# Two groups of small attention products a unit, and 48 weight columns in the state update of later units

## The chip, the cores and the metric

The kernel runs on one NeuronCore of one Trainium2 chip. The metric is device time in microseconds, from the first to the last instruction of a run with what the device adds around it; lower is better. The core has five instruction queues that matter here: TensorE (PE, with its weight loads shown as PEld), VectorE (DVE), ScalarE (ACT), GpSimd (POOL) and SyncE (SP), which issues the DMAs. Each works off its own queue in order; semaphores tie them together.

## The reference

Two blocks follow one another, all in fp32. The first is a gated linear attention (4 batches, 8 heads, 768 steps, 48 channels a head):

```python
f = 1.0 / (1.0 + np.exp(-f_logit))
for t in range(S):
    state = f[:, :, t, :, None] * state + einsum('bhd,bhe->bhde', k[:, :, t], v[:, :, t])
    y[:, :, t] = einsum('bhd,bhde->bhe', q[:, :, t], state)
```

Its heads are laid side by side to x of 4 x 768 x 384. The second is a mixer: a low-rank product along the sequence (`u = x + (x^T U V)^T`, rank 32), then `u + relu(u @ w_ch1) @ w_ch2` with 1536 hidden channels.

## The kernel before

**Units.** The attention is computed in 16 units, each one batch and two heads (`par` 0 and 1, in partitions 0 to 47 and 64 to 111; each head has 64 places, PAD, for its 48 channels, D). A unit has 12 chunks of 64 steps. Units 0 to 3 are batch 0, 4 to 7 batch 1, 8 to 11 batch 2, 12 to 15 batch 3.

A unit n goes through two sets of steps. `prepare(n)` makes its operands, mostly on DVE and ACT: gates (transpose of f_logit, sigmoid), keep (a DVE scan from the end of each chunk, L694; the ACT copy `least`, L699, comes behind it), keys (k transposed and multiplied), read-back (a DVE scan, L712) and queries (q transposed and multiplied into qT). From unit 6 on the transposes are DVE's.

`attend(n)` does the products, with small matmuls of 48 or 64 rows and up to 64 columns, of which four can stand in the array at once:

- scores (`sc`, L788): 48 matmuls, and then DVE's multiplication with the causal mask to A (L795).
- kept (`pt`, L809): 12 transposes of the keys, copied by ACT to kb (L815); ACT also spreads the chunk decays to `whole` (L813).
- states (`ds`, L825): 48 matmuls with kb as weights (64 columns a head, of which 48 are channels) and v; ACT copies the result to `added` (L831).
- scan (L846): a DVE scan over `added` and `whole`, which carries the state from chunk to chunk; for batches 1 to 3 ACT then copies it to st in another order (L851).
- read (`y`, L863): 44 matmuls of qT with st, and a tiny ACT copy of the last columns of y to `seen` (L870).
- inner (`y`, L881): 48 matmuls of A with v onto the same y, in reverse order of blocks, so that the first of them writes what `seen` reads and has to wait for it; ACT copies y to x (L887).

**The order around the change.** `steps` yields, for n = 5 and so on, ten pieces: scores of unit n-1, kept of n, gates, keep and keys of n+1, read of n-1, states and scan of n (one piece), read-back and queries of n+1, and inner of n-1. `attention` calls a `Fill` before each piece. The fill holds the mixer work of the batch before, in pieces with a cost each, and issues them in equal portions by cost: for batch 1's units the second layer of batch 0's mixer (`po`, L283), for batches 2 and 3 the first layer (`pz`, L258: 12 full matmuls a piece, then an ACT relu, L268) and the products of a fast two by two scheme for the second layer (`pw`, L312, with DVE additions, L187). A portion need not hold a whole piece; then two small groups meet on PE.

PE's queue is in the order in which the pieces are called. DVE's and ACT's are too, up to the start of batch 1's mixer; after that a planner orders these two by priority, where the mask, the state scan and the mixer's additions are marked urgent. PSUM has three buffers of two banks for the small groups (`big`) and two of one bank for pz, po and pw (`mm`). In batch 3 `beside` also issues 14 DVE additions of weights (L743), two behind each piece from the 21st on. `start_mixer` runs between the batches: the low-rank product of the batch just finished, with what is left of the fill.

Batch 0's units have an order of their own and come before. After batch 3 the last mixer products run alone (`pp`, L410, and `pw`).

Of the kernel before, what the change touches and what calls it, by code (L numbers as in the profile page):

```python
# [21 lines left out]
PAD = 64  # L22
# [450 lines left out]
def factored_path(ctx, tc, q, k, v, f_logit, moe_U, moe_V, moe_w_ch1, moe_w_ch2, out, ok):  # L473
# [4 lines left out]
    nc = tc.nc  # L478
    B, H, S, D = q.shape
    P = nc.NUM_PARTITIONS  # L480
# [3 lines left out]
    NBL = S // P  # L484
# [45 lines left out]
    def load(n, *names):  # L530

        b, hp = divmod(n, HP)
        for nm in names:
            if nm == "v":
                v_tiles[n] = three.tile([P, NBL, 2, D], F32, name="v_nat")
            for par in range(2):
                head = src[nm][b, 2 * hp + par]
                if nm == "v" and par:

                    for s in range(2):  # L540
                        nc.sync.dma_start(
                            out=v_tiles[n][(1 - s) * C : (2 - s) * C, :, par, :],
                            in_=head.rearrange("(c s p) d -> s p c d", s=2, p=C)[s],
                        )
                    continue
                if nm == "v" or n < TURNED:
                    dst = v_tiles[n] if nm == "v" else nat[n % 2][nm]
                    nc.sync.dma_start(out=dst[:, :, par, 0:D], in_=head.rearrange("(c p) d -> p c d", p=P))
                    continue
                head = head.rearrange("(c i) d -> i c d", i=NB)  # L550
                for part in range(2):
                    p0 = par * PAD + part * NB
                    n_ch = min(NB, D - part * NB)
                    nc.sync.dma_start(
                        out=raw[n % 2][nm][p0 : p0 + NB, :].rearrange("p (c d) -> p c d", d=NB)[:, :, 0:n_ch],
                        in_=head[:, :, part * NB : part * NB + n_ch],
                    )
# [38 lines left out]
    added = const.tile([P, D * NCH + 1], F32, name="added")  # L596
# [173 lines left out]
    def attend(n):  # L770

        b, hp = divmod(n, HP)
        T = units[n]
        vt = v_tiles[n]
        rows = [slice(par * PAD, par * PAD + D) for par in range(2)]
        chunk = [slice(c * C, (c + 1) * C) for c in range(NCH)]

        part = [slice(s * C, (s + 1) * C) for s in range(2)]
# [37 lines left out]

        def states():

            ds = ps_big.tile([P, 2, 512], F32, name="ds", tag="big")
            for c in range(NBL):  # L820
                for s in range(2):
                    for par in range(2):

                        i = (c + (s & par)) % NBL
                        nc.tensor.matmul(  # L825
                            ds[par * PAD : (par + 1) * PAD, s, c * D : (c + 1) * D],
                            lhsT=T["kb"][part[s ^ par], par, i, :], rhs=vt[part[s ^ par], c, par, :],
                            start=True, stop=True,
                        )

            nc.scalar.copy(  # L831
                added[:, 1:].rearrange("p (e c s) -> p e c s", c=NBL, s=2),
                ds[:, :, 0 : NBL * D].rearrange("p s (c e) -> p e c s", e=D),
            )

        def scan():

            st = T["st"] = two.tile([P, NCH, D], F32, name="st")
            by_e = "p (e c) -> p c e"
            if b == 0:  # L840
                states = st.rearrange("p c e -> p (c e)")
                T["st"] = states.rearrange(by_e, c=NCH)
            else:
                states = added[:, 0 : D * NCH]
            with tc.high_priority(offset=AHEAD):
                nc.vector.tensor_tensor_scan(  # L846
                    states, added[:, 0 : D * NCH], T["whole"].rearrange("p e c -> p (e c)"), 0.0, ALU.add, ALU.mult
                )
                if b > 0:

                    nc.scalar.copy(st, states.rearrange(by_e, c=NCH))  # L851
# [20 lines left out]
        def inner():  # L872
# [18 lines left out]
            del units[n], v_tiles[n]  # L891

        return [kept, states, scan, scores, read, inner]

    ahead, here = {}, {}

    def front(n, *names):

        if n >= NU:
            return []  # L900
        if n not in ahead:
            ahead[n] = dict(zip(("gates", "keep", "keys", "read_back", "queries"), prepare(n)))
        return [ahead[n].pop(nm) for nm in names]

    def rear(n, *names):

        if not 0 <= n < NU:
            return []
        if n not in here:
            here[n] = dict(zip(("kept", "states", "scan", "scores", "read", "inner"), attend(n)))  # L910
        return [here[n].pop(nm) for nm in names if nm in here[n]]

    def steps(first, last):


        for n in range(first, last):
            yield from rear(n - 1, "scores") + rear(n, "kept") + front(n + 1, "gates", "keep", "keys")
            yield from rear(n - 1, "read")
            made = rear(n, "states", "scan")
            yield lambda: [f() for f in made]  # L920
            yield from front(n + 1, "read_back", "queries") + rear(n - 1, "inner")
            if n + 2 < NU:
                load(n + 2, "v")

# [30 lines left out]
    with tc.manual_schedule(engines={nc.vector.engine, nc.scalar.engine}):  # L955
# [51 lines left out]

        EARLY = 6
        second = chain(front(HP, "gates", "keep", "keys", "read_back", "queries"), steps(HP, 2 * HP + 1))
        for i, (_, piece) in enumerate(start + m.firsts[1:]):  # L1010
            piece()
# [6 lines left out]
        n = len(m.seconds) // (NBL // 2)  # L1018
# [6 lines left out]
    for b in range(2, B - 1):  # L1025
        todo, after = m.main, m.after
        attention(steps(b * HP + 1, (b + 1) * HP + 1), 10 * HP, todo)
        m = start_mixer(b, after)

    pieces = beside(steps((B - 1) * HP + 1, NU + 1), 10 * (HP - 2), [lambda i=i: sum_of_w(i) for i in range(len(W_SUMS))])  # L1030
    todo = m.first(0) + m.ready(0) + m.second(0)
    attention(pieces, 29, todo[:-1])
# [316 lines left out]
@with_exitstack  # L1349
def kernel(  # L1350
    ctx: ExitStack,
    tc: tile.TileContext,
    q: bass.AP,
    k: bass.AP,
    v: bass.AP,
    f_logit: bass.AP,
    moe_U: bass.AP,
    moe_V: bass.AP,
    moe_w_ch1: bass.AP,
    moe_w_ch2: bass.AP,  # L1360
    out: bass.AP,
):


    nc = tc.nc
    args = (q, k, v, f_logit, moe_U, moe_V, moe_w_ch1, moe_w_ch2, out)
    flag = ctx.enter_context(tc.tile_pool(name="flag", bufs=1))
    ok = flag.tile([1, 1], I32, name="ok")
    with ExitStack() as inner:
        factored_path(inner, tc, *args, ok)  # L1370
    good = nc.values_load(ok[0:1, 0:1], min_val=0, max_val=1)
    with tc.If(good == 0):
        with ExitStack() as inner:
            general_path(inner, tc, *args)
# [30 lines left out]
```

## Time and profile before

| | |
|---|---|
| Timed runs, median (lowest, highest) | 489.46 us (487.31, 491.5) |
| Span of the profiled execution | 486.9 us |
| PE busy / DVE busy / ACT busy | 469.2 / 355.4 / 163.2 us |
| sc, ds and inner matmuls | 768 each, about 220 ns one |
| read matmuls / kept transposes | 704 / 192 |
| `added` copies | 16, 641 ns each |
| state scans | 16, 1350 ns each |
| pz matmuls / pw matmuls | 504, 383 ns / 756, about 328 ns |

For the profiled execution the page gives its span, from the first to the last instruction; no other total of it is recorded. It lies 0.4 us below the lowest timed run and 2.5 below the median.

To read the views: PE, PEld, DVE, ACT, POOL and SP are the engines; L825 is a line of the kernel; `ds<-v_nat,kb` is what an instruction writes and reads; `64*64` is the part of the array that a matmul takes; `x48` is how many were merged. A bracket at the end tells the idle time of the engine ahead of the group and what ended it. Matmuls overlap, so a block's length is read from its start to the start of the next, not from the sum of durations.

### The profile page before, as it was taken

The page shows a single profiled execution, that of the slowest core. Times are in us where ns is not written, and L with a number is a line of the kernel's source. Part 1 is how long each engine was busy: PE and PEld are TensorE (multiplying, and loading weights), DVE is VectorE, ACT ScalarE, POOL GpSimd, SP SyncE. Part 2 cuts the span into 40 slices and gives each one's busy share as a digit, 9 for nine tenths or more (in the row PEclk, how much of TensorE's full clock was granted, in tenths as well). Part 3 has the DMA queues.
Part 4 walks back from the last instruction along what each step waited for, and adds up shares of the span by engine and source line. Part 5 has one row for each costly group of instructions (what it writes and reads, how often), then busy time and mean ns, then how long its engine had stood idle before and what let it go on. Part 6 is the DMA issues. An engine that isn't in the chain of part 4 may idle for free.

```text
span 486.9 us, 12734 instructions
## 1 busy us (share of the span) xinstructions
PE 469.2 (96%) x5541; PEld 400.0 (82%) x5541; DVE 355.4 (73%) x563; ACT 163.2 (34%) x309; POOL 37.6 (8%) x49
## 2 busy tenths in 40 slices
PE   7996899999999999999999999999999999999995
PEld 4775688886566568899898888899979999999995
DVE  5887689777999857656857548797896886958642
ACT  2444666664334313423231403433231312112200
POOL 3002245453000000000000000000000000000000
PEclk9999999999999999999999999999999999999999
DMA  9979975756778512333535100100000000000001
GB/s 146 158 153 178 254 194 135 162 143 79 110 116 121 96 41 36 52 48 67 76 55 94 25 18 18 27 3 20 19 1 1 33 2 18 16 1 34 1 33 38
DMA packets 158679, 34.34 MB, mean 71 GB/s; under 512 B 149206, under 2 KB 157078, under 8 KB 158614
## 3 DMA queue, kind: packets, MB, share of 16 engines
q1 hardware_dynamic: 158614, 33.44, 37.0%
q8 instruction: 45, 0.74, 0.6%
q14 instruction: 20, 0.16, 0.1%
HBM read 28.70 MB, written 4.72 MB: 69 GB/s over the span
## 4 chain that ended last, share of the span: by engine, by line
PE 79%; DVE 10%; DMA 3%; issue 3%; ACT 2%; SPq 2%; DVEq 0%; ACTq 0%
PE pw L312 26%; PE pz L258 23%; PE pp L410 11%; PE y L863 2%; PE pt L660 2%; PE sc L788 2%; PE ds L825 2%; PE y L881 2%; PE po L283 2%; PE idle L962 2%; PE put L246 1%; DMA late<-in_f_logit_dram 1%; DVE late L694 1%; DVE late L712 1%; PE pt L809 1%
## 5 line engine op out<-in xcount | busy, mean ns | idle before, releaser
L258 PE MATMUL pz<-uT,w 128*128 128x256 f32 x504 | 115.7, 383 | 0.3 <-ACT uT L247 0.3
L258 PEld LDWEIGHTS pz<-uT,w 128*128 128x128 f32 x504 | 93.4, 190 | 13.3 <-issue 0.5
L312 PE MATMUL pw<-w,z_all 128*128 128x192 f32 x216 | 37.7, 329 | 0.0
L312 PE MATMUL pw<-zw,w_raw 128*128 128x192 f32 x216 | 37.4, 327 | 0.0
L312 PEld LDWEIGHTS pw<-zw,w_raw 128*128 128x128 f32 x216 | 35.2, 190 | 0.8 <-issue 0.6
L312 PEld LDWEIGHTS pw<-w,z_all 128*128 128x128 f32 x216 | 35.0, 190 | 0.7
L95 POOL TENSOR_TENSOR w<-w_y,w_r 128x384 int32<-128x384 int32 x24 | 31.5, 1311 | 41.5 <-DVE w_y L94 36.5
L694 DVE TENSOR_TENSOR_SCAN late<-fz,late 128x768 f32<-128x768 f32 x16 | 28.1, 1755 | 8.9 <-ACT fz L689 4.2
L268 ACT ACTIVATE z_all<-pz 128x512 f32<-128x512 f32 x33 | 19.7, 596 | 41.4 <-PE pz L258 41.3
L410 PE MATMUL pp<-v_nat,late 128*128 128x128 f32 x224 | 28.8, 275 | 0.0
L712 DVE TENSOR_TENSOR_SCAN late<-fz,other 128x768 f32<-128x768 f32 x16 | 27.9, 1745 | 0.1
L410 PEld LDWEIGHTS pp<-v_nat,late 128*128 128x128 f32 x224 | 27.0, 192 | 0.0
L283 PE MATMUL po<-w,zw 128*128 128x384 f32 x72 | 25.6, 499 | 0.0
L283 PE MATMUL po<-w,z_all 128*128 128x384 f32 x72 | 25.3, 496 | 0.3 <-DVE o L187 0.3
L403 ACT ACTIVATE other<-other 128x512 f32<-128x512 f32 x18 | 11.3, 631 | 39.9 <-DVE other L187 39.9
L851 ACT COPY st<-added 128x576 f32<-128x576 f32 x12 | 14.7, 1224 | 27.5 <-DVE added L846 27.5
L92 DVE TENSOR_SCALAR w_y<-w_y 128x384 f32<-128x384 f32 (+3 forms) x27 | 13.1, 485 | 14.0 <-ACT w_y L90 13.8
L795 DVE TENSOR_TENSOR A<-sc,causal 128x768 f32<-128x768 f32 x16 | 15.2, 947 | 10.7 <-PE sc L788 10.7
L283 PEld LDWEIGHTS po<-w,z_all 128*128 128x128 f32 x72 | 13.1, 190 | 8.7 <-DVE o L187 0.9
L283 PEld LDWEIGHTS po<-w,zw 128*128 128x128 f32 x72 | 12.9, 189 | 8.7 <-issue 1.2
L187 DVE TENSOR_TENSOR w_raw<-z_all 128x768 f32<-128x768 f32 x12 | 11.4, 954 | 10.6 <-ACT z_all L268 9.2
L312 PE MATMUL pw<-w,other 128*128 128x192 f32 x108 | 18.6, 327 | 0.0
(193 smaller groups left out, 825.6 us busy)
## 6 DMA issues: line engine op xcount, KB each, us to landing
w_raw<-in_moe_w_ch_dram SPq DMA_DIRECT2D x18, 384.0 KB, 3.9
out_dram<-o SPq DMA_DIRECT2D x24, 192.0 KB, 1.9
v_nat<-in_v_dram SPq DMA_DIRECT2D x16, 144.0 KB, 3.6
v_nat<-in_v_dram SPq DMA_DIRECT2D x32, 72.0 KB, 3.3
zw<-in_moe_w_ch_dram SPq DMA_DIRECT2D x6, 384.0 KB, 5.7
late<-in_f_logit_dram SPq DMA_DIRECT2D x10, 96.0 KB, 3.1
late<-in_k_dram SPq DMA_DIRECT2D x10, 96.0 KB, 3.0
late<-in_q_dram SPq DMA_DIRECT2D x10, 96.0 KB, 2.6
```

Source lines behind the costliest of these rows:

```text
L92: nc.vector.tensor_scalar(f, f, SMALLEST, LARGEST, ALU.max, ALU.min)
L95: nc.gpsimd.tensor_tensor(dst.bitcast(I32), shaped(y.bitcast(I32)), shaped(r), ALU.add)
L187: nc.vector.tensor_tensor(*args)
L258: nc.tensor.matmul(pm[:, i * 2 * P : (i + 1) * 2 * P], lhsT=w1[:, m, o : o + P], rhs=uT[a][:, m, :], start=(m == 0), stop=(m == NDC - 1))
L268: nc.scalar.activation(z[a, c][:, k : k + 2, :].rearrange("p i t -> p (i t)"), pm, AF.Relu)
L283: nc.tensor.matmul(pm, lhsT=z[a, i // NI][:, i % NI, s * P : (s + 1) * P], rhs=w2[:, i, :], start=(i == 0), stop=(i == NFC - 1))
L312: nc.tensor.matmul(pm[:, n * HM : (n + 1) * HM], lhsT=lhs[:, i, :], rhs=rhs[:, i, :], start=(i == 0), stop=(i == NI - 1))
L410: nc.tensor.matmul(pm[:, i, r * P : (r + 1) * P], lhsT=room["w"](wn)[:, r * P : (r + 1) * P], rhs=x_node(a, xn), start=((xn, wn) == of[0]) ...
L694: nc.vector.tensor_tensor_scan(backwards(X, S - 1, S), backwards(f, S, S), backwards(ends, S - 1, S), 0.0, ALU.mult, ALU.add,)
L712: nc.vector.tensor_tensor_scan(Y, f[:, 0:S], starts, 0.0, ALU.mult, ALU.add)
L795: nc.vector.tensor_tensor(T["A"], sc[:, :, 0 : NBL * C].rearrange("p h (c i) -> p h c i", i=C), causal.unsqueeze(1).unsqueeze(1).broadcast ...
L851: nc.scalar.copy(st, states.rearrange(by_e, c=NCH))
```

## The change

Two edits, both in the factored path. `steps` no longer yields scores and kept as two pieces and read, inner, states and scan as three; a new helper `joined` puts such steps into one piece, preceded by empty pieces, so that the count of portions for the fill stays the same in a full iteration. The joined piece is issued at the place of the last of its parts, and the fill's portions that stood between the parts now come ahead of it. Inner, which came last, moves ahead of states. At the last iteration there is one piece fewer than before.

For batches 1 to 3 the states matmuls take 48 columns of kb as weights, so ds has 48 rows a head. The copy to `added` is done for each head apart, because the 16 rows between are not written any more; they keep what batch 0 left there, and nothing reads their results.

```diff
@@ -816,6 +816,7 @@
 
         def states():
 
+            M = D if b else PAD
             ds = ps_big.tile([P, 2, 512], F32, name="ds", tag="big")
             for c in range(NBL):
                 for s in range(2):
@@ -823,15 +824,16 @@
 
                         i = (c + (s & par)) % NBL
                         nc.tensor.matmul(
-                            ds[par * PAD : (par + 1) * PAD, s, c * D : (c + 1) * D],
-                            lhsT=T["kb"][part[s ^ par], par, i, :], rhs=vt[part[s ^ par], c, par, :],
+                            ds[par * PAD : par * PAD + M, s, c * D : (c + 1) * D],
+                            lhsT=T["kb"][part[s ^ par], par, i, 0:M], rhs=vt[part[s ^ par], c, par, :],
                             start=True, stop=True,
                         )
 
-            nc.scalar.copy(
-                added[:, 1:].rearrange("p (e c s) -> p e c s", c=NBL, s=2),
-                ds[:, :, 0 : NBL * D].rearrange("p s (c e) -> p e c s", e=D),
-            )
+            for r in rows if b else [slice(0, P)]:
+                nc.scalar.copy(
+                    added[r, 1:].rearrange("p (e c s) -> p e c s", c=NBL, s=2),
+                    ds[r, :, 0 : NBL * D].rearrange("p s (c e) -> p e c s", e=D),
+                )
 
         def scan():
 
@@ -910,15 +912,20 @@
             here[n] = dict(zip(("kept", "states", "scan", "scores", "read", "inner"), attend(n)))
         return [here[n].pop(nm) for nm in names if nm in here[n]]
 
+    def joined(*groups):
+
+        groups = [g for g in groups if g]
+        for _ in groups[1:]:
+            yield lambda: None
+        yield lambda: [f() for g in groups for f in g]
+
     def steps(first, last):
 
-
         for n in range(first, last):
-            yield from rear(n - 1, "scores") + rear(n, "kept") + front(n + 1, "gates", "keep", "keys")
-            yield from rear(n - 1, "read")
-            made = rear(n, "states", "scan")
-            yield lambda: [f() for f in made]
-            yield from front(n + 1, "read_back", "queries") + rear(n - 1, "inner")
+            yield from joined(rear(n - 1, "scores"), rear(n, "kept"))
+            yield from front(n + 1, "gates", "keep", "keys")
+            yield from joined(rear(n - 1, "read"), rear(n - 1, "inner"), rear(n, "states", "scan"))
+            yield from front(n + 1, "read_back", "queries")
             if n + 2 < NU:
                 load(n + 2, "v")
```

## The prediction

> **What bounds the kernel now.** I read the busy shares first, then the table of stretches, then the order of time on each engine where the attention units run. Batch 1's units run from 108 to 169 us, batch 2's in 181 to 293, batch 3's in 293 to 336; afterwards there is no attention.
>
> ```profile
> span 486.9 us, 12734 instructions
> ...
> PE 469.2 (96%) x5541; PEld 400.0 (82%) x5541; DVE 355.4 (73%) x563; ACT 163.2 (34%) x309; POOL 37.6 (8%) x49
> ```
> ```profile
> 108.00:169.00 61.00, 60.07 (x888) 37.38 (x886) 54.01 (x69) 24.90 (x49) 5.32 (x4) 1.00 0.72 109
> 181.00:293.00 112.00, 111.86 (x1311) 98.04 (x1310) 71.59 (x95) 35.14 (x65) 0.00 (x0) 1.00 0.34 54
> 293.00:336.00 43.00, 42.74 (x890) 37.82 (x889) 34.91 (x54) 16.53 (x28) 0.00 (x0) 1.00 0.07 17
> ```
>
> The columns after the stretch's length are PE, PEld, DVE, ACT, POOL. In batches 2 and 3 PE never rests: every nanosecond taken from or added to its queue is time. In batch 1 PE (60.07 of 61) and DVE (54.01) are both nearly full, and the chain that ended last runs over DVE there from 113 to 167 us, by way of its scans and transposes. So batch 1 has two masters and needs its own sum.
>
> The price of a break between small and full matmuls is in the order of time on PE (start, duration, instruction):
>
> ```profile
> 203.56 2.86 PE L258 MATMUL pz<-uT,w 128*128 128x256 f32 x12
> 206.35 0.93 PE L788 MATMUL sc<-qT,kz 48*64 48x64 f32 x48
> 207.21 2.86 PE L258 MATMUL pz<-uT,w 128*128 128x256 f32 x12
> ...
> 218.50 0.84 PE L863 MATMUL y<-st,qT 48*64 48x48 f32 x42
> ...
> 219.19 0.91 PE L825 MATMUL ds<-v_nat,kb 64*64 64x48 f32 x46
> 220.04 2.22 PE L312 MATMUL pw<-w,z_all 128*128 128x192 f32 x12
> ```
>
> Twelve pz after a small group last 2.79 (203.56 to the next start); a pair of such pieces lasts 5.38 (197.34 to 202.72), so the piece that follows a full one takes 2.59. Leaving a small group costs 0.20. Read and ds side by side last 1.54 (218.50 to 220.04); alone they take 0.84 (192.87 to 193.71) and 0.85 (196.49 to 197.34). Entering costs 0.15. A removed break is **0.35**, and **0.20** between sc and kept, which take 1.38 together and 0.86 + 0.52 apart.
>
> The other price is a wait that inner has behind read: ScalarE must copy `seen` in between (L870). Only the last unit has them side by side in this part:
>
> ```profile
> 333.87 0.90 PE L863 MATMUL y<-st,qT 48*64 48x48 f32 x44
> 334.81 0.16 ACT L870 COPY seen<-y 128x2 f32<-128x2 f32 x1 [2.98 <-PE y L863]
> 335.03 0.91 PE L881 MATMUL y<-v_nat,A 64*64 64x48 f32 x48 [0.26 <-ACT seen L870]
> ```
>
> Inner starts 1.16 after read, with ACT free. Read beside a group that does not wait takes 0.67 (218.50 to about 219.17). The stall is **0.49**.
>
> Batch 1's cycle, where DVE sets the pace:
>
> ```profile
> 129.54 1.76 DVE L694 TENSOR_TENSOR_SCAN late<-fz,late 128x768 f32<-128x768 f32 x1 [0.90 <-ACT fz L689]
> ...
> 132.73 0.96 DVE L675 TENSOR_TENSOR kz<-kz,late 128x768 f32<-128x768 f32 x1
> 133.61 1.35 DVE L846 TENSOR_TENSOR_SCAN added<-added,whole 128x576 f32<-128x576 f32 x1
> ```
> ```profile
> 131.33 0.21 ACT L699 COPY least<-late 128x12 f32<-128x12 f32 x1 [1.71 <-DVE late L694]
> 131.45 0.16 ACT L870 COPY seen<-y 128x2 f32<-128x2 f32 x1
> 131.50 0.65 ACT L831 COPY added<-ds 128x576 f32<-128x576 f32 x1
> ```
>
> Call T the end of the keep scan (131.30). ACT stands at `least` until T; seen and the added copy come behind it, though PE had read and ds ready at 128.8. DVE takes up the added scan at T + 2.31, with no idle time before it. A cycle is 12.05 (133.61 to 145.66).
>
> [...] In the trace the ds matmuls start in rounds of four, one round each 58 ns, so weights of 64 columns can be the limit; nothing in it shows 48. [...] the added copies of 576 elements take 641 ns here and follow one another every 0.53.
>
> **The change part by part.** The sequence follows from the fill's costs and shares, carried through both versions of `steps`; for before it is the order of the trace.
>
> *Batch 2 (units 8 to 11).* Before: 20 small groups stand in 16 blocks, since reads, ds, sc and inner sometimes meet (two pairs worth 0.35, two worth 0.20: 1.1). After: 8 blocks, four joints of 0.20 and eight of 0.35: 3.6. Gain 2.5. Against it four seen stalls, 4 x 0.49 = 1.96. ACT is free then: the relu of the fill before read starts 0.1 after read and takes 0.60, read needs 0.94. Narrower weights: 12 rounds x 13 ns = 0.16 a unit, bounds 0 and 0.16, I take 0.16, four units 0.64. Sum **-1.2**.
>
> *Batch 3 (units 12 to 15).* Before, thin fill already lets groups meet: 18 groups in 9 blocks (seven joints of 0.35, two of 0.20: 2.85), among them ds between read and inner for units 13 and 14, which hides seen. After: 7 blocks, eight of 0.35, three of 0.20: 3.4. Gain 0.55; three new stalls 1.47 (unit 15 had its own); weights 3 x 0.16. Sum **+0.4**.
>
> *Batch 1 (units 4 to 7).* 15 blocks become 8 (2.0 off PE), but DVE's added scan is what matters. Now ds(n) stands behind inner(n-1), inner behind seen, seen behind `least`. From T: seen at T + 0.15, inner at T + 0.36 (131.66 in the trace), ds 0.74 later at T + 1.10. Ds start to added copy is 1.04 (196.49 to 197.53), 0.88 with narrower weights: T + 1.98. The x copy, 0.98 behind inner's start, slips in before. Two added copies end 0.53 + 0.64 later, T + 3.15, and the scan can start there instead of T + 2.31: **0.84 a cycle**. In the first cycle DVE had some slow small operations (scan at T + 2.90): 0.27. In the third, the fill puts five po pieces (1.94 each) instead of four between the ds of one unit and the read of the next, so PE comes to read 1.1 us after DVE frees seen: about 2.0. Sum 0.27 + 0.84 + 2.0 + 0.84 = **+3.9**, of which the batch's end gives back 0.3 (PE's wait for DVE at 169.34). What queues behind DVE's scan: the read-back scan, qT, the mask A and the next unit's gates, all on one queue. PE's gain of 2.0 is lost: DVE ends last.
>
> *The second added copy* in batches 2 and 3 hides in DVE's and ACT's slack (DVE 71.59 of 112). If that cover is gone, st's copy and the relu behind it are 0.5 late; a pz needs one of two PSUM buffers, and the third pz after a joined group would start when that relu ends. Only unit 9's step has three in a row: I allow 0.3. One call of fill less at the end moves nothing: the rest is issued there anyway. x is complete two portions earlier before each mixer: nothing waited for it.
>
> Sum: -1.2 + 0.4 + 3.6 + 0.3 = **+3.1** on a span of 486.9, that is 490.0. No total beside the span is recorded; the median of the runs, 489.46, stands 2.5 above it, the lowest run 0.4. On the median: **492.6**.
>
> **Rivals.** *A, faster:* PE is the master of batch 1 too (60.07 of 61), and DVE absorbs the late scan by its 0.90 wait for fz in each cycle. Then PE's own balance counts: 2.0 + 0.64 less four stalls 1.96 plus the 0.93 it waits for seen today, -1.6; total -2.4 + 0.3, **487.4**. For it: the busy share. Against: the fz wait lies on DVE's own chain (transpose, sigmoid, scan) and moves with it. It decides if ds lands before T + 1.4. *B, much slower:* ACT. St's copy waits in ACT's queue for the scan, which waits for the copies, which wait for inner; relus behind it hold pz's buffers. If every one of seven units in batches 2 and 3 loses 0.7 that way, +5: **497.6**. For it: st waited up to 4.1 us in unit 14. Against: the pieces behind are seldom three pz. *C, the narrow weights bring nothing,* rounds being set by issue: 11 x 0.16 back, **494.4**.
>
> **Chances.** Forecast 0.5, A 0.15, B 0.2, C 0.15. Range 487.5 to 498: it takes in A's end and B. No change and 1% (4.9 us, what a measurement of this kernel can tell) leave: faster 0.04, within 0.60, slower 0.36.
>
> **What would show it.** Right: two small blocks a unit; 0.26 idle "<-ACT seen" before each inner; the added scan of batch 1 idle for ACT added, near 0.8 each; batch 2 no longer than 112; batch 1's end near 172.6 instead of 169. Wrong: rounds of ds still 58 ns apart; DVE without idle time at the added scan; pz waiting for a relu.

## The result and the profile after

The changed kernel takes 495.47 us (median of four runs, 493.8 to 497.22) against 488.44 for the kernel before (four runs): +7.0 us. The ratio is 1.0131, with a 95% interval of 1.0096 to 1.0166, so it is 1.3% slower, give or take 0.35%. The profiled executions differ by 5.6 us. The head and the first part of the page after:

```profile
span 492.5 us, 12757 instructions
...
PE 466.7 (95%) x5541; PEld 399.7 (81%) x5541; DVE 356.9 (72%) x563; ACT 172.4 (35%) x321; POOL 37.7 (8%) x49
```

PE is busy for 2.5 us less than before, and the span is 5.6 longer: PE did save work, and lost more to waiting. ACT has 12 instructions more, the second added copies (7.6 us in sum), and is busy for 9.2 us more. To find the place, I cut the span at marks of PE's order that every variant has: the first ds of unit 4, the first transposes of batch 1's mixer (`put`, L246), those of batch 2's mixer, and the last transpose of the attention (`lp`). From there to the end of PE all variants take 145.6 us. Starts on PE at these marks, in the kernel after:

```profile
93.90 0.76 PE L826 MATMUL ds<-v_nat,kb 64*48 64x48 f32 x48
...
183.05 2.13 PE L246 MATMUL put<-ident,x 128*128 128x128 f32 x18
...
296.18 2.13 PE L246 MATMUL put<-ident,x 128*128 128x128 f32 x18
...
341.41 0.27 PE L1076 MATMUL lp<-ident,low 128*1 128x128 f32 x1
```

Batch 1 thus takes 183.05 - 93.90 = 89.15 us (84.53 before), batch 2 113.13 (112.43), batch 3 45.23 (44.57): **+4.62, +0.70 and +0.66**. What lies ahead of the first mark differs by up to 4.6 us between the profiles (93.01 to 97.65 us), and the cuts leave it out.

The four added scans of batch 1, before and then after; then PE in the first unit and ACT in the second, after:

```profile
121.56 1.35 DVE L846 TENSOR_TENSOR_SCAN added<-added,whole 128x576 f32<-128x576 f32 x1
...
133.61 1.35 DVE L846 TENSOR_TENSOR_SCAN added<-added,whole 128x576 f32<-128x576 f32 x1
...
145.66 1.35 DVE L846 TENSOR_TENSOR_SCAN added<-added,whole 128x576 f32<-128x576 f32 x1
...
157.71 1.35 DVE L846 TENSOR_TENSOR_SCAN added<-added,whole 128x576 f32<-128x576 f32 x1
```
```profile
121.08 1.36 DVE L848 TENSOR_TENSOR_SCAN added<-added,whole 128x576 f32<-128x576 f32 x1 [0.21 <-ACT added L833]
...
134.88 1.36 DVE L848 TENSOR_TENSOR_SCAN added<-added,whole 128x576 f32<-128x576 f32 x1 [1.60 <-ACT added L833]
...
148.88 1.36 DVE L848 TENSOR_TENSOR_SCAN added<-added,whole 128x576 f32<-128x576 f32 x1 [1.86 <-ACT added L833]
...
161.87 1.36 DVE L848 TENSOR_TENSOR_SCAN added<-added,whole 128x576 f32<-128x576 f32 x1 [0.85 <-ACT added L833]
```
```profile
113.84 0.90 PE L865 MATMUL y<-st,qT 48*64 48x48 f32 x44
118.24 0.91 PE L883 MATMUL y<-v_nat,A 64*64 64x48 f32 x48 [3.49 <-ACT seen L872]
118.97 0.72 PE L826 MATMUL ds<-v_nat,kb 64*48 64x48 f32 x48
119.62 5.83 PE L283 MATMUL po<-w,zw 128*128 128x384 f32 x12
```
```profile
130.91 0.21 ACT L699 COPY least<-late 128x12 f32<-128x12 f32 x1 [1.71 <-DVE late L694]
131.78 0.16 ACT L872 COPY seen<-y 128x2 f32<-128x2 f32 x1 [0.65 <-PE y L865]
132.97 0.64 ACT L889 COPY x<-y 128x576 f32<-128x576 f32 x1 [1.03 <-PE y L883]
133.56 1.28 ACT L833 COPY added<-ds 48x576 f32<-48x576 f32 x2
```

DVE now stands at all four added scans, for 4.52 us in sum, where before it took them without idle time: that is nearly all of the batch's +4.62. The chain is readable from the last fence: `seen`, then x, then the two added copies, each behind PE's inner and ds. In this unit `seen` waits not for `least` but for PE (0.65): read itself came late. Two things in the second fence were not in the prediction: a wait of 3.49 us for seen in the first unit, and two po pieces (12 matmuls) that last 5.76 (119.62 to the next group at 125.38) where they take 4.07 elsewhere. TensorE's granted clock, which the profile gives as a share of full speed, is 0.50 from 119.72 to 123.13 us, and 3.41 us at half speed fit the 1.7 more.

### The profile page after: what moved, and what is told of

The parts are those of the page before. It is cut to its first block, busy times and chain, and to the rows that moved or that the text cites. A ratio compares the mean times of both kernels' runs of the same rounds, so it can differ in the third digit from the quotient of the medians.

```text
span 492.5 us, 12757 instructions
## 1 busy us (share of the span) xinstructions
PE 466.7 (95%) x5541; PEld 399.7 (81%) x5541; DVE 356.9 (72%) x563; ACT 172.4 (35%) x321; POOL 37.7 (8%) x49
## 4 chain that ended last, share of the span: by engine, by line
PE 78%; DVE 10%; ACT 4%; DMA 3%; issue 3%; SPq 2%; DVEq 0%; ACTq 0%
PE pw L312 25%; PE pz L258 18%; PE pp L410 11%; PE po L283 6%; PE y L883 3%; PE y L865 2%; PE sc L788 2%; PE pt L660 2%; PE idle L969 2%; PE ds L826 2%; PE put L246 1%; DVE late L694 1%; PE pt L809 1%; SPq L554 1%; DMA late<-in_f_logit_dram 1%
## 5 line engine op out<-in xcount | busy, mean ns | idle before, releaser
L258 PE MATMUL pz<-uT,w 128*128 128x256 f32 x504 | 114.1, 382 | 1.7 <-ACT z_all L268 1.2
L712 DVE TENSOR_TENSOR_SCAN late<-fz,other 128x768 f32<-128x768 f32 x16 | 28.0, 1747 | 0.1
L283 PE MATMUL po<-w,zw 128*128 128x384 f32 x72 | 26.8, 521 | 0.0
L92 DVE TENSOR_SCALAR w_y<-w_y 128x384 f32<-128x384 f32 (+3 forms) x27 | 14.1, 522 | 12.1 <-ACT w_y L90 11.8
L283 PEld LDWEIGHTS po<-w,zw 128*128 128x128 f32 x72 | 14.0, 202 | 10.2 <-issue 2.7
L883 PE MATMUL y<-v_nat,A 64*64 64x48 f32 x768 | 14.6, 221 | 7.8 <-ACT seen L872 7.8
```

Of the source, the lines that this page charges most:

```text
L92: nc.vector.tensor_scalar(f, f, SMALLEST, LARGEST, ALU.max, ALU.min)
L258: nc.tensor.matmul(pm[:, i * 2 * P : (i + 1) * 2 * P], lhsT=w1[:, m, o : o + P], rhs=uT[a][:, m, :], start=(m == 0), stop=(m == NDC - 1))
L283: nc.tensor.matmul(pm, lhsT=z[a, i // NI][:, i % NI, s * P : (s + 1) * P], rhs=w2[:, i, :], start=(i == 0), stop=(i == NFC - 1))
L712: nc.vector.tensor_tensor_scan(Y, f[:, 0:S], starts, 0.0, ALU.mult, ALU.add)
L883: nc.tensor.matmul(o(s, par, c), lhsT=T["A"][part[s ^ par], par, c, :], rhs=vt[part[s ^ par], c, par, :], start=False, stop=True, skip_gro ...
```

## The experiments

Each was run beside the kernel before, on the same chip as it. The edits are shown against the change. The table has the length of the three batches in each profiled execution, cut as above, and the ratio to the kernel before.

| kernel | batch 1 | batch 2 | batch 3 | ratio (95%) |
|---|---|---|---|---|
| before | 84.53 | 112.43 | 44.57 | |
| the change | 89.15 | 113.13 | 45.23 | 1.0131 (1.0096 to 1.0166) |
| weights_only | 84.54 | 111.79 | 44.08 | 0.9977 (0.9959 to 0.9994) |
| groups_only | 89.44 | 113.13 | 45.45 | 1.0113 (1.0082 to 1.0143) |
| ds_first | 85.38 | 110.92 | 43.56 | 0.9973 (0.9955 to 0.9990) |
| batch1_old | 84.53 | 113.15 | 45.22 | 1.0033 (1.0017 to 1.0049) |
| best | 84.51 | 110.91 | 43.54 | 0.9952 (0.9927 to 0.9977) |
| after_busy | 90.94 | 113.63 | 45.22 | 1.0169 (1.0137 to 1.0202) |
| after_st_pool | 91.36 | 112.54 | 44.98 | 1.0162 (1.0126 to 1.0199) |
| best_st_pool | 84.56 | 109.69 | 43.76 | 0.9952 (0.9923 to 0.9981) |
| after_busy5 | 88.32 | 113.15 | 45.22 | 1.0092 (1.0060 to 1.0124) |
| first_old | 91.18 | 113.14 | 45.23 | 1.0154 (1.0119 to 1.0188) |

My theory was that the loss lies in the order read, inner, ds: inner's wait for seen is exposed on PE, and in batch 1 it pushes ds, and with it DVE's scan, behind `least`. The rival was the second added copy.

**weights_only**: the old order of pieces, with the 48 columns and the two copies.

```diff
-            yield from joined(rear(n - 1, "scores"), rear(n, "kept"))
...
+            yield from rear(n - 1, "scores") + rear(n, "kept") + front(n + 1, "gates", "keep", "keys")
+            yield from rear(n - 1, "read")
+            made = rear(n, "states", "scan")
+            yield lambda: [f() for f in made]
+            yield from front(n + 1, "read_back", "queries") + rear(n - 1, "inner")
```

> Only the 48 columns and the two added copies, in the old order of pieces. Order theory (the loss lies in where inner and its seen wait stand): a ds block falls from 0.85 to 0.65 us, the second copy hides, about -1.4 us in batches 2 and 3 and nothing in batch 1: ratio 0.997 to 0.998, span 485 to 486. Copy theory (the second added copy on ScalarE is what delays the scan): 2 us or more slower, ratio 1.004 or higher, with idle time of the added scan <- ACT added in batch 1.

Measured: 0.9977; batch 1 unchanged to 0.01 us, batch 2 -0.64, batch 3 -0.49. These are four and three units at 0.16, the figure of the prediction (1.1 in sum, a little less than the 1.4 expected). In the trace the rounds of four ds matmuls start 45 ns apart instead of 58, as in the change: the 13 ns a round that the prediction took, when no trace had shown them yet. The copy theory falls: the second copy costs nothing in the old order.

**groups_only**: the two groups alone.

```diff
-            M = D if b else PAD
+            M = PAD
...
-            for r in rows if b else [slice(0, P)]:
+            for r in [slice(0, P)]:
```

> Only the two groups; 64 columns and one added copy as in the kernel before. Order theory: most of the loss stays. In batch 1 the scan waits 0.47 a cycle instead of 0.84 (one copy less, ds 0.16 longer), 1.6 in the third, so 2.6 to 3 there, and about 1.5 in batches 2 and 3: +4 to +5 us, ratio 1.008 to 1.010. Copy theory: within 1 us of the kernel before.

Measured: 1.0113, batch 1 +4.91, batch 2 +0.70, batch 3 +0.88. By the batches all of the loss is here, with one added copy, so the copy theory falls on this side too. But batch 1 loses 2 us more than I had said: the fourth scan waits 0.37, near the 0.47 said, the others 0.93, 1.13 and 2.02. In this profile the half clock lasts 6.8 us (from 115.81), and inner and ds of the first unit run in it: they take 1.31 and 1.43 us from start to start, 0.73 and 0.81 in the next unit.

**ds_first**: in the joined piece, states and scan go ahead of inner.

```diff
-            yield from joined(rear(n - 1, "read"), rear(n - 1, "inner"), rear(n, "states", "scan"))
+            yield from joined(rear(n - 1, "read"), rear(n, "states", "scan"), rear(n - 1, "inner"))
```

> The change with states and scan ahead of inner in the joined piece: read, ds, inner. Order theory: ds hides seen (0.65 us of work against 0.49), so no PE wait <- ACT seen but for the last unit, and the added scan of batch 1 no longer waits for ACT: batch 1 as before, batches 2 and 3 some 4 us shorter than before the change but for relu waits of up to 1.5: ratio 0.991 to 0.996. Copy theory: the two copies still delay the scan, no faster than before. Rival of thick blocks (operands asked for later, so that PE waits elsewhere): slower than before by 2 us or more.

Measured: 0.9973, and the batches are 3.77, 2.21 and 1.67 us shorter than in the change. One swap of two groups takes back all of the loss and more, with the same number of blocks on PE. Of batch 1's added scans only the third still waits, behind the five po pieces:

```profile
145.60 1.36 DVE L848 TENSOR_TENSOR_SCAN added<-added,whole 128x576 f32<-128x576 f32 x1 [1.10 <-ACT added L833]
```

In batch 3 seen is hidden but for unit 15, and the saving is 3 x 0.49 and 0.2. Batch 1 did not come back whole (85.38 against 84.53), which I had expected; 1.10 of scan wait is its reason. The ratio missed the 0.991 to 0.996 expected: batches 2 and 3 together are 2.5 us shorter than before, not 4.

**batch1_old**: the old pieces for batch 1, the change for the rest.

```diff
+            if n <= 2 * HP:
+                yield from rear(n - 1, "scores") + rear(n, "kept") + front(n + 1, "gates", "keep", "keys")
+                yield from rear(n - 1, "read")
...
+            else:
+                yield from joined(rear(n - 1, "scores"), rear(n, "kept"))
```

> Batch 1's units in the old order of pieces, later ones as in the change; 48 columns throughout. If batch 1 is where the time goes, as the two traces say (+4.2 to +4.6 of +5.6), +1 to +1.5 us is left, ratio 1.001 to 1.004, with the relu wait of 1.2 us in batch 2 still there. If the loss is spread over all units alike, two thirds of it stay: ratio 1.008 or higher.

Measured: 1.0033, batch 1 at 84.53 as before, batches 2 and 3 as in the change to 0.02 us. The batches do not act on one another, so their differences may be added.

**best**: batch1_old and ds_first together.

> Batch 1 in the old order of pieces, batches 2 and 3 joined with states and scan ahead of inner, 48 columns. If the stages add up as in the runs so far (batch 1 as before the change, batch 2 110.9 us, batch 3 43.6), 2.4 us less than the kernel before: ratio 0.994 to 0.996. If batch 1's order matters to the batches behind it, no better than ds_first: 0.997.

Measured: 0.9952 (0.9927 to 0.9977), each batch equal to its part's to 0.02 us. It is the fastest order tried, 2.3 us below the kernel before and some 9 below the change.

The next three runs ask whether the half clock at 119.72 us is what makes PE late for the second cycle. In the change PE stands idle for 3.49 us, up to 118.24, and the clock is half for 3.41 us, from 119.72 to 123.13.

**after_busy**: the change, with dummy matmuls in the first seen wait.

```diff
         def inner():
             y = T["y"]
+            if n == HP:
+                idle_too = ps_big.tile([P, 2, 512], F32, name="idle_too", tag="big")
+                for _ in range(9):
+                    nc.tensor.matmul(idle_too[:, 0, 0:DM], lhsT=ident, rhs=ends[:, 0:DM], start=True, stop=True)
```

> The change, with nine full dummy matmuls on PE between read and inner of unit 4 (extra work, into a PSUM tile of its own), so that PE is not idle in its longest seen wait. Clock theory (3.5 us of idle PE halve its granted clock for the 3.4 us that follow, which makes PE late for the second cycle): no half clock behind 118 us, the second added scan waits 0.8 instead of 1.6, batch 1 some 0.7 us shorter than the change. Rival (PE is late in the second cycle for another reason, the clock costs nothing): batch 1 as in the change, the second scan still waits 1.6.

Measured: batch 1 at 90.94, longer. The nine took 6.0 us; each stands in the trace as two matmuls of 0.33. They ended after the wait they were to fill, and the first scan waited 2.65. The second waited 0.85, as the clock theory said, but behind a DVE that was late by 2.4 it could not be told from the rival. Hence a second try:

**after_busy5**: the same with five (`range(5)`).

> As after_busy, with five dummy matmuls: nine took 6.0 us and ran 2.5 us past the wait that they were to fill, so the first added scan came 2.4 us later and the second was measured against a DVE that was late. Five take 3.3 us and end before seen does. Clock theory: first scan waits about 0.2 as in the change, second 0.8 to 0.9 instead of 1.6, batch 1 0.6 to 0.8 us shorter than the 89.15 of the change. Rival: second scan still 1.6, batch 1 unchanged.

Measured: batch 1 at 88.32, 0.83 shorter than in the change, the ratio 1.0092. Only the second scan's wait changed:

```profile
121.90 1.36 DVE L848 TENSOR_TENSOR_SCAN added<-added,whole 128x576 f32<-128x576 f32 x1 [0.21 <-ACT added L833]
134.89 1.36 DVE L848 TENSOR_TENSOR_SCAN added<-added,whole 128x576 f32<-128x576 f32 x1 [0.85 <-ACT added L833]
```

Useless work made batch 1 shorter, and the granted clock is where the two profiles part. (The ratios agree in direction, but their intervals, 1.0060 to 1.0124 here and 1.0096 to 1.0166 in the change, overlap.) Two stretches of 2 us behind the wait, of the change (columns: length, PE, PEld, DVE, ACT, POOL, the granted clock, DMA), and then the stretch from 117 to 133 us of after_busy5:

```profile
120.00:122.00 2.00, 2.00 (x4) 1.07 (x4) 1.79 (x2) 1.03 (x2) 0.00 (x0) 0.50 0.36 57
122.00:124.00 2.00, 2.00 (x6) 1.01 (x4) 2.00 (x2) 1.53 (x2) 0.00 (x0) 0.72 0.77 93
```
```profile
117.00:133.00 16.00, 14.80 (x303) 9.60 (x305) 14.69 (x19) 5.91 (x13) 2.31 (x1) 1.00 0.58 88
```

**first_old**: the old pieces for batch 1's first full iteration only (`if n <= HP + 1:` in batch1_old's edit).

> The change, with the first full iteration of batch 1 (scores of unit 4 to inner of unit 4) in the old order of pieces, so that PE fills its wait for seen with po. Clock theory: no half clock; first scan without wait, second 0.8 to 0.9, third 1.9, fourth 0.8: batch 1 about 88.1, 1 us shorter than the change. Rival: second scan 1.6 as in the change.

Measured: batch 1 at 91.18, slower than the change. Neither side had it right: the long wait did not go away but moved to the next unit, where PE again arrived early, and the clock was half there, for 6.8 us from 131.82 on.

```profile
128.39 0.90 PE L865 MATMUL y<-st,qT 48*64 48x48 f32 x44
132.61 1.53 PE L883 MATMUL y<-v_nat,A 64*64 64x48 f32 x48 [3.32 <-ACT seen L872]
133.92 1.18 PE L826 MATMUL ds<-v_nat,kb 64*48 64x48 f32 x48
135.03 5.91 PE L283 MATMUL po<-w,zw 128*128 128x384 f32 x12
```

Inner and ds themselves are slowed here (0.74 and 0.65 in the change, 1.31 and 1.11 here, from start to start), and the second and third scans wait 1.90 and 3.54. It is a failed experiment on its own question and one more case of the half clock beside a long wait.

**after_st_pool** and **best_st_pool**: st's copy of batches 2 and 3 on GpSimd.

```diff
-                    nc.scalar.copy(st, states.rearrange(by_e, c=NCH))
+                    if b > 1:
+                        nc.gpsimd.tensor_copy(st, states.rearrange(by_e, c=NCH))
+                    else:
+                        nc.scalar.copy(st, states.rearrange(by_e, c=NCH))
```

> The change, with the copy to st of batches 2 and 3 on GpSimd instead of ScalarE. ACT queue theory (the relu that frees pz's buffer stands behind st's copy, which waits for a scan that DVE takes late): PE's wait for ACT z_all in batch 2 falls from 1.2 to 0.3 us or less, batch 2 about 1 us shorter. Rival (DVE's late scan itself, by way of `whole`, or a GpSimd copy so slow that read waits for it): batch 2 as in the change or longer.

They aim at the one new wait of batch 2. In the change, behind the joined group of unit 9:

```profile
208.17 1.35 DVE L848 TENSOR_TENSOR_SCAN added<-added,whole 128x576 f32<-128x576 f32 x1
...
209.56 1.21 ACT L853 COPY st<-added 128x576 f32<-128x576 f32 x1 [3.31 <-DVE added L848]
210.79 0.60 ACT L268 ACTIVATE z_all<-pz 128x512 f32<-128x512 f32 x1
...
211.44 2.86 PE L258 MATMUL pz<-uT,w 128*128 128x256 f32 x12 [1.22 <-ACT z_all L268]
```

DVE takes the four sums for the next `pw` and qT ahead of the scan (202.96 to 208.2), the scan releases st's copy, and the relu that frees pz's PSUM buffer is queued behind it. With the copy on GpSimd, batch 2 is 0.59 shorter and the wait falls from 1.22 to 0.68: about half of what I expected. What is left goes, as I read the trace, the rival's way: `whole` (L813) waits for the same scan and stands ahead of the relu too. The ratio, 1.0162, cannot show this: 0.59 us is 0.1% of the time, and its interval is 0.7% wide. In the profiled execution batch 1 took 91.36, with the half clock for 6.8 us: inner, ds and the two po pieces of its first unit take 1.31, 1.11 and 6.08 us there, 0.73, 0.65 and 4.07 in the next.

> As best, with the copy to st of batches 2 and 3 on GpSimd. ACT queue theory: batch 2 loses its last relu wait of 0.43, so 0.3 to 0.5 us less than best. If DVE and GpSimd hinder each other, DVE's operations beside the copy grow and it is no faster than best or slower.

Batch 2 came down to 109.69, by more than I expected (1.2 against 0.3 to 0.5), while batch 3 is 0.22 longer than in best. But the ratio is that of best, 0.9952; a gain of that size over best isn't settled by these runs. Of DVE and GpSimd side by side, after_st_pool's profile shows one case: st's copy of unit 9 takes 2.53 us on GpSimd (the other six 1.20 to 1.99), and DVE's read-back scan (L712), which starts 0.21 us ahead of it, takes 1.73, as the first three of batch 1 do.

## Why the prediction was right or wrong

It said slower, 492.6 on the median, range 487.5 to 498; measured 495.47. The direction and the main place were right: batch 1, because ds came to stand behind seen. The size was too small: 3.1 against 7.0 by the medians and 6.0 by the three batches (4.62 + 0.70 + 0.66). Of the 2.9 that the batches had more, 1.0 is batch 1's (3.6 forecast), 1.6 batch 2's (-0.9) and 0.3 batch 3's. Two things speak less for it: its chances gave 0.60 to a difference within 1% and only 0.36 to slower, and its range was wide enough to take in two of its rivals.

- **Breaks on PE, the seen stall, the weights.** Right. Inner starts 1.16 to 1.17 after read in every unit of batches 2 and 3, PE's bracket shows 0.26 `<-ACT seen` each time, as here for unit 9, and two blocks a unit stand in the trace. The weights gave 0.16 a unit in a run of their own. Rival C falls with that.

```profile
227.50 0.90 PE L865 MATMUL y<-st,qT 48*64 48x48 f32 x44
228.66 0.91 PE L883 MATMUL y<-v_nat,A 64*64 64x48 f32 x48 [0.26 <-ACT seen L872]
```

- **Batch 1, the added scan.** Right in mechanism and nearly in size, but for one term. I had 0.27, 0.84, 2.0 and 0.84; DVE waits 0.21, 1.60, 1.86 and 0.85. With PE kept busy (after_busy5) it is 0.21, 0.85, 1.86 and 0.85, so the working held for all four within 0.15. Part of that is luck. The prediction let the second added copy start 0.53 after the first, a step that the trace before shows from the x copy to `whole` (124.08 to 124.61) but not between added copies, and end 0.64 later; in the change they start 0.65 apart and take 1.28 together, so each, on 48 partitions, takes the 0.64 that the one copy took on 128. But the first of them starts at T + 1.88 (119.76, with T at 117.88) and not at T + 1.98, so the scan still begins at T + 3.2, where 3.15 was forecast. The 0.75 more in the second wait goes with the half clock (119.72 to 123.13 us) behind PE's idle stretch of 3.49 us; in after_busy5, where dummy work fills the stretch and the granted clock is 1.00, it is gone. The prediction let inner wait for `seen` in the first unit and put no cost on what follows an idle PE. What brings the half clock on is not shown (last section).
- **The 0.3 given back at the end of batch 1.** Wrong. PE's wait for `o` grew from 0.28 to 0.95: DVE's delay passed to PE whole.
- **Batch 2, -1.2 and an allowance of 0.3.** The -1.2 is what is left when the two waits below are taken out of +0.70. The allowance was mis-sized. After unit 9's group the three pz pieces last 9.46 (204.77 to 214.23) where they need 3 x 2.59 + 0.20 = 7.97: 1.49. I had counted the second added copy's 0.5 and not that DVE's order itself would change: as I read the trace, with read two portions later qT waits for it, and the sums are taken ahead of the scan. A further 0.45 stands at the pz of 267.46; it starts after DVE's additions behind the keep scan have ended (267.31), but the profile names no such wait, so that cause is not shown. Together 1.9 instead of 0.3.
- **Batch 3.** +0.66 against +0.4; 0.24 of it is one pair of pz (314.30 to 319.92, 5.62 for 5.38).
- **Rival A** (faster) falls: ds_first shows that batch 1's time follows DVE's scan, ds ended at T + 1.81 at the earliest and not before T + 1.4, and DVE's wait for fz, which was to absorb the delay, stands at 0.90 as before. **Rival B** happened in one unit out of seven.

```profile
129.12 1.76 DVE L694 TENSOR_TENSOR_SCAN late<-fz,late 128x768 f32<-128x768 f32 x1 [0.90 <-ACT fz L689]
```

What stays open: the medians differ by 1 us more than the three batches. The timed executions carry no trace, but each has its mean granted clock on record: 0.984 to 0.996 for the four of the change (mean 0.990, the profiled one 0.996), and a mean of 0.995 for 59 executions of the kernel before (the profiled one 0.998). In the traces of the change and of the kernel before the clock is either 1.00 or 0.50, so that is an estimated 9.6 us at half clock in the change's executions against 4.1 in its profile, and 5.0 against 1.5 for the kernel before. In the 59, each microsecond at half clock goes with 0.33 us more time. By this estimate some 0.7 of the 1 us is half clock that the profiles happened not to catch; with four executions it is no more than an estimate.

## What to carry to other kernels

Before two small groups are put side by side, look for what the second waits for from the first: a wait that other work covered is bare once nothing stands between (0.26 us of PE in each unit of batches 2 and 3 here), and every group queued behind it inherits it. Here the number of blocks was not the question but the order in the block; with an independent group put between the two (read, ds, inner) the kernel is 0.3% faster than before, and 0.5% with batch 1 left in the old order. The narrow weights alone bring 0.2% of that; the joining itself gains 1.4 us in batches 2 and 3 (best against weights_only, by their profiles) and costs 0.8 in batch 1 (ds_first against weights_only). Where two engines are both nearly full, make the sum for each of them; here PE's 2.5 us less of busy time did not pay for the 4.52 us that DVE stood at its added scans.

## What the runs showed of the hardware that was not expected

In batch 1 of four profiles the granted clock was 0.50 in or behind a long idle stretch of PE. In the change the stretch lasted 3.49 us, up to 118.24, and the clock was half from 119.72 to 123.13; in groups_only, after_st_pool and first_old, with stretches of 3.47, 3.48 and 3.32 us, it was half for 6.8 us. In ds_first, with 2.95 us of idle time up to 117.78, all windows from 112 to 132 us show 1.00. The 3.4 us of half clock cost 1.7 us on PE and 0.75 of the next scan's wait, 0.83 of batch 1. With five dummy matmuls on zeros and ones, 3.3 us in the idle stretch, the window from 117 to 133 us shows 1.00. The loss lands on the next unit, where the trace shows a wait for PE and none for a clock.

What brings the half clock on is not shown, and the length of the idle stretch is not enough to tell. In the change the clock fell 1.48 us after the stretch had ended; in groups_only it fell inside it, 1.80 us after its start (115.81, start at 114.01), in first_old 2.53 after its start (131.82 and 129.29). And the clock is not full all the time in profiles without such a stretch: the mean granted clock of the profiled execution is 0.990 in weights_only and 0.992 in batch1_old, an estimated 9.8 and 7.8 us at half clock, though PE's longest waits there are 2.7 us (its first matmul's, for `ident`), 1.7 and 1.4, the windows from 112 to 132 us show 1.00, and batch 1 is as long as before to 0.01 us.
